# A block of sliding-window attention and a gated MLP: w_out's pieces made on GpSimd, w_in's second part in its own buffers, an inversion moved by one step, and the last two tiles' transposes inside products

## Chip, cores and metric

One core of one Trainium2 chip. The metric is the device time of one execution in microseconds (us), as the median of a few runs; profiles give a span (first to last instruction) on the same core.

## What is computed

Cut to what matters, for S = 2048 tokens of width D = 640, 32 heads of 20, a window of 256 and a hidden width of 2 x 864:

```python
h  = x + attention(layernorm(x)) @ wo        # causal, window 256, 32 heads
z  = gelu(layernorm(h) @ w_in)               # 2048 x 1728
z1, z2 = z[:, :864], layernorm(z[:, 864:])
g  = w_sp @ z2 + b_sp[:, None]               # a 2048 x 2048 matrix over the tokens
h2 = h + (z1 * g) @ w_out
```

All in fp32. The kernel takes one precise product as three: each operand is split into a high part, rounded to fp32r, and a low part, the operand less the high part, and hi·hi + hi·lo + lo·hi are summed.

## The kernel before

**Tiles and stages.** The tokens are 16 tiles of 128 (NT). The work goes through these stages, with the times of the profiled execution: v, q, k and attention (to about 462 us); the output projection with the second layernorm (to 550); z1, the first half of the hidden layer, by `z_pair` for eight pairs of tiles (550 to 641); z2 by `z2_pair` for pairs 8 to 12 (641 to 698); the first gates, which multiply w_sp's one half by the z2 that is ready (`first_gate`, 698 to 832); z2 of pairs 13 to 15 (832 to 868); the second gates, with the product by w_out between them (`second_gate`, 868 to 1116).

z1 and the gates use a scheme of seven block products in place of eight. Its right-hand pieces B11, T1, T2, B22, T3, B21 and T4 are made from four blocks by `right_blocks` (L724): high parts by copies on ScalarE (ACT, recorded at the helper's L720), low parts and block differences by subtractions on VectorE (DVE, L714).

**Who sets the order.** Up to the end of attention the order on each engine is that of the program. Behind `ms.close()` the framework's scheduler, with a timeline of its own, sets the order of every engine and of the DMA issues, so an edit there can shift many rows. Loads and stores are nearly all issued by SyncE (SP), some by GpSimd (POOL). Each engine works through its instructions in order. `steps` holds the matmul groups of the later stages, and `at(n, f)` places f at step n; `run(n)` does what is placed there and then step n.

**w_in's first half.** `win1_prep` (L771) makes the pieces of w_in for z1 while the projection's tiles pass: one `next` of it after each tile, two after each odd one. wraw is one buffer of [128, 2, 2, 432]. `load_win1(0, b)` puts the k-rows 0 and 2 of w_in there early (L208 to 210); after their pieces, rows 1 and 3 are loaded over them (`load_win1`, recorded at L193), and then row 4 (L783). Around them on ACT and DVE stand the projection's own operations for tile i: the layernorm's sums and its result hn(i) (L1249 to L1257), the split xb of the attention output for the tile after the next (L171 to L174), and ho, the copy of the transposed tile out of the bank ht_ps (L841 the transposes on PE, L720 the copy).

**The inversion.** `inverse_sums(c)` (L376) loads the softmax sums of 512 tokens from o_d, takes their reciprocals and stores these to r_d, from where `load_o`'s `load_rs` (L153) loads them spread over the partitions, as the factor for the attention output (`norm_o`, L163). It is a generator that takes one `next` in each step of attention: for c = 0 the reciprocal comes at the fourth. `proj_early(s)` places the first tiles' loads and splits into the last steps of attention; at s = 121 it loads both the outputs and the inverses of pair 1.

**w_out.** `second_gate(0)` loads the seven row blocks of w_out (128 x 640 each) into stage and row3, and splits each there: the high part by ACT (L136), the low part by DVE (L137), into e1["wout"], which lies in memory that the z2 weights hold until the last `z2_pair`. `staged_pieces` (L999) is work of the same kind that POOL already does in the first gates: it loads blocks of z2, makes their pieces in stage by a cast and a subtraction, and stores them to zp_d.

**The end.** `turn_y(n, dst)` (L1113) transposes tile n's z1·g and splits it into dst; `project` (L1126) multiplies by w_out; `final(n)` (L1139) adds h and stores. After the last step: `turn_y(14)`, `final(14)`, `turn_y(15)`, the last projection out_l.

## Time and profile before

| what | us |
|---|---|
| runs, median (lowest, highest) | 1122.15 (1116.82, 1125.29) |
| profiled execution, its own time | 1121.05 |
| its span | 1119.3 |
| TensorE (PE) busy | 1088.3 |
| DVE busy | 715.4 |
| ACT busy | 573.9 |
| POOL busy | 336.4 |
| DMA, mean rate over the span | 162 GB/s |

In the profile's timeline a row is: start, duration, engine, line, operation, out<-in, count, and in brackets how long the engine had stood idle before it and what ended that. A row of the list of waits is: waiting instruction <- releaser: total us, times, longest. A row of a table of stretches is: stretch, its length, then busy us (and instructions) of PE, of PE's weight loads, of DVE, ACT and POOL, the granted TensorE clock, the share of time that the DMA engines were busy, and GB/s. The names of the buffers are cut: wraw, zl (pieces of w_in, later of z2), aw (left-hand pieces), fx (loads of w_sp and of transposed tiles), m (attention outputs on their way to the projection).

### The profile page before, as it was taken

To read this page: it belongs to the slowest core of one execution; us is meant where nothing else is said; L and a number is where in the kernel's file an instruction comes from. 1 tells how busy PE (TensorE), PEld (TensorE's weight loads), DVE (VectorE), ACT (ScalarE), POOL (GpSimd) and SP (SyncE) were. 2 spreads that over 40 slices of the span, in tenths; PEclk is the share of its full clock that TensorE was granted. 3 is DMA by queue.
4 is the path that set the end of the run, shared out by engine and by line. 5 is a ranking of instruction groups with operands and counts; after the bars stand their busy time and mean duration, and the time that the engine had idled before them with its cause. 6 is when DMAs were issued, how large, how long until landed. Compare 5 with 4: busy or idle time off the path is not lost.

```text
span 1119.3 us, 27705 instructions
## 1 busy us (share of the span) xinstructions
PE 1088.3 (97%) x10667; PEld 976.1 (87%) x10667; DVE 715.4 (64%) x2038; ACT 573.9 (51%) x1222; POOL 336.4 (30%) x492
## 2 busy tenths in 40 slices
PE   8999999999999999989999999999999999999998
PEld 7998877668777887789989999999989899999998
DVE  6541113889999998676567478565538975566542
ACT  4334333259888999566766566433336521222210
POOL 3114444457666778401100155333101000000000
PEclk9999999999999999999999999999999999999999
DMA  7213665666666663588665421545571664444331
GB/s 259 74 33 102 171 218 165 204 208 196 194 198 192 209 194 119 170 277 288 226 200 177 151 76 38 182 153 197 177 248 38 202 182 140 124 135 148 99 95 59
DMA packets 86692, 182.44 MB, mean 163 GB/s; under 512 B 11552, under 2 KB 47904, under 8 KB 82640
## 3 DMA queue, kind: packets, MB, share of 16 engines
q1 hardware_dynamic: 82864, 169.46, 47.3%
q0 software_dynamic: 1392, 5.97, 1.6%
q10 hardware_dynamic: 2304, 5.24, 1.2%
q8 instruction: 84, 1.38, 0.5%
q14 instruction: 48, 0.39, 0.1%
HBM read 119.54 MB, written 62.29 MB: 162 GB/s over the span
## 4 chain that ended last, share of the span: by engine, by line
PE 59%; DMA 5%; DVE 4%; ACT 2%; issue 1%; SPq 1%; POOL 1%; DVEq 0%; ACTq 0%; POOLq 0%
PE g L1091 22%; PE out_ps L1130 8%; PE zb L953 7%; PE pv L432 5%; PE bank L338 4%; PE bank L404 4%; PE wo_ps L95 2%; PE zx L901 2%; PE zv L901 1%; PE zy L901 1%; PE yt_ps L1119 1%; DMA wraw<-w_in_in 1%; DMA fx<-w_in_in 1%; DVE zl L714 1%; DMA m<-r_d 1%
## 5 line engine op out<-in xcount | busy, mean ns | idle before, releaser
L407 ACT ACTIVATE pt<-bank 128x384 f32<-128x384 f32 (+2 forms) x512 | 200.2, 492 | 14.7 <-PE bank L404 10.9
L1091 PE MATMUL g<-zl,aw 128*128 128x432 f32 x768 | 172.4, 359 | 1.8 <-DVE zl L714 1.2
L720 ACT ACTIVATE aw<-fx 128x512 fp32r<-128x512 f32 (+2 forms) x160 | 93.0, 595 | 156.2 <-PE g L1091 98.7
L350 DVE CUSTOM_DVE_ANT_0 junk<-bank,strip 128x288 bf16<-128x288 f32 x392 | 157.7, 454 | 3.9 <-PE bank L338 2.4
L1091 PEld LDWEIGHTS g<-zl,aw 128*128 128x128 f32 x768 | 143.3, 188 | 9.1 <-DVE zl L714 1.8
L1091 PE MATMUL g<-ze,aw 128*128 128x432 f32 x576 | 133.8, 361 | 1.4 <-ACT aw L720 0.7
L432 PE MATMUL pv<-pt,v_sb 128*32 128x192 f32 (+3 forms) x1984 | 127.5, 321 | 3.0 <-DVE ot L448 1.3
L714 DVE TENSOR_TENSOR aw<-fx,aw 128x512 fp32r<-128x512 f32 (+2 forms) x152 | 98.7, 658 | 27.0 <-ACT aw L720 26.1
L1091 PEld LDWEIGHTS g<-ze,aw 128*128 128x128 f32 x576 | 107.2, 188 | 7.9 <-ACT aw L720 1.5
L404 PE MATMUL bank<-slot 123*32 123x288 bf16 (+5 forms) x1536 | 107.0, 280 | 2.8 <-ACT pt L407 1.3
L409 POOL TENSOR_SCALAR_AFFINE_SELECT pt<-pt 128x512 f32<-128x512 f32 x128 | 82.4, 644 | 49.6 <-ACT pt L407 48.5
L1130 PE MATMUL out_ps<-wout,y_sp 128*128 128x320 f32 (+1 forms) x630 | 95.9, 309 | 0.4 <-ACT y_sp L136 0.4
L953 PE MATMUL zb<-win,aw 128*128 128x432 f32 x480 | 95.4, 359 | 0.0
L1130 PEld LDWEIGHTS out_ps<-wout,y_sp 128*128 128x128 f32 (+1 forms) x630 | 94.0, 188 | 1.2 <-ACT y_sp L136 0.7
L953 PEld LDWEIGHTS zb<-win,aw 128*128 128x128 f32 x480 | 89.9, 188 | 4.9 <-DVE aw L714 0.4
L338 PE MATMUL bank<-slot 120*32 120x288 bf16 (+2 forms) x1264 | 87.7, 283 | 2.2 <-issue 1.2
L538 DVE TENSOR_TENSOR rest<-qk,sg 128x512 f32<-128x512 f32 x40 | 27.6, 691 | 86.5 <-ACT sg L536 86.5
L412 POOL TENSOR_SCALAR_AFFINE_SELECT pt<-pt 128x512 f32<-128x512 f32 x112 | 73.4, 655 | 0.0
L404 PEld LDWEIGHTS <-slot 123*32 123x32 bf16 x1536 | 53.6, 96 | 17.8 <-issue 6.9
L432 PEld LDWEIGHTS pv<-pt,v_sb 128*32 128x32 f32 x1984 | 60.2, 110 | 9.0 <-POOL pt L412 3.7
L541 POOL TENSOR_TENSOR sg<-rest,sg 128x512 bf16<-128x512 f32 x40 | 46.6, 1164 | 69.7 <-ACT sg L540 62.1
L714 DVE TENSOR_TENSOR row<-g,row 128x432 f32<-128x432 f32 x80 | 47.9, 602 | 27.9 <-PE g L1091 22.5
(210 smaller groups left out, 2158.3 us busy)
## 6 DMA issues: line engine op xcount, KB each, us to landing
fx<-wsp_in SPq DMA_DIRECT2D x32, 512.0 KB
slot<-qk_d SPq DMA_DIRECT2D x72, 200.0 KB
qk_d<-sg SPq DMA_DIRECT2D x32, 384.0 KB
slot<-qk_d SPq DMA_DIRECT2D x72, 160.0 KB
fx<-hn_d SPq DMA_DIRECT2D x32, 320.0 KB
o_d<-ot SPq DMA_DIRECT2D x64, 128.0 KB
z_d<-row SPq DMA_DIRECT2D x18, 432.0 KB
g_d<-row SPq DMA_DIRECT2D x16, 432.0 KB
```

Of the source, the lines that this page charges most:

```text
L338: nc.tensor.matmul(ps[32 * j:32 * j + 32, :n], part(st, half, 120, 0, hh, q0, 32), part(st, half, 120, 1, hh, lo + skip * j, n), start=Tru ...
L350: nc.vector.tensor_tensor_reduce(out=junk[:, :n], in0=ps[:, :n], in1=keep, scale=1.0, scalar=NEG, op0=OP.add, op1=OP.max, accum_out=m_cols ...
L404: nc.tensor.matmul(ps[32 * i:32 * i + 32, b:e], part(st, half, 123, 1, hh, k0, 32), part(st, half, 123, 0, hh, kb * P + b, e - b), start=T ...
L407: nc.scalar.activation(pt[:, hh, :n], ps[:, :n], AF.Exp, scale=SCALE)
L409: nc.gpsimd.affine_select(out=pt[:, :, :P], in_=pt[:, :, :P], pattern=[[0, 4], [1, P]], base=0, channel_multiplier=-1, compare_op=OP.is_ge ...
L412: nc.gpsimd.affine_select(out=pt[:, :, 256:], in_=pt[:, :, 256:], pattern=[[0, 4], [-1, P]], base=-1, channel_multiplier=1, compare_op=OP. ...
L432: nc.tensor.matmul(ps[32 * hh:32 * hh + 32, a - 512 * c:b - 512 * c], v_sb[:, kb, v0:v0 + 32], pt[:, hh, a - kb * P:b - kb * P], start=fir ...
L714: (eng or nc.vector).tensor_tensor(out=out, in0=a, in1=b, op=op)
L720: nc.scalar.activation(out, a, AF.Copy)
L953: nc.tensor.matmul(b[0][:, :HF], a[t][:, x, kk], win2[0][:, y, kk, h * HF:(h + 1) * HF], start=kk + x + y == 0, stop=kk == KD - 1 and x == 1)
L1091: nc.tensor.matmul(ps, w[m][x][:, k], zc[k][m][:, y], start=start and k + x + y == 0, stop=stop and k == 3 and x == 1, skip_group_check=True)
L1130: nc.tensor.matmul(ps[j][:, :HD], src[:w, a, k, :], e1["wout"][:w, b, k, j * HD:(j + 1) * HD], start=(k == 0 and a + b == 0), stop=(k == K ...
```

## The change

The diff, cut to its core:

```diff
+    wout_d = dram.tile([P, 2, KF * D], F32, name="wout_d")
...
+    ones = const.tile([P, 2], F32, name="ones")
...
-    def load_win1(k, b):
-        src = w_in[:, :FH].rearrange("k (h c) -> k h c", h=2)
-        r = (k + 2 * b) * P
-        nc.sync.dma_start(mem["wraw"][:, b], src[r:r + P])
+    def load_win1(b):
+        nc.sync.dma_start(mem["wraw"][:, b], w_in[2 * b * P:(2 * b + 1) * P, :FH].rearrange("k (h c) -> k h c", h=2))
...
         if s == 121:
-            for f in load_o(1)[:2]:
-                f()
+            tiles, mem["rs"], _ = load_o(1)
+            tiles()
             mem["invert"]()
         if s == 122:
+            mem["rs"]()
             norm_o(0, nc.vector)
...
-            for _ in range(5 if c else 3):
+            for _ in range(5 if c else 4):
                 yield
...
-            copy(pieces()[m][:, 0], raw[m])
+            nc.scalar.activation(pieces()[m][:, 0], raw[m], AF.Copy, scale=one)
...
-        return rows[i % 4][:, :D] if i > 11 else view(fx, (i % 4 - 2 + i // 9 * 2) * D, D)
+        if i == NT - 1:
+            return stage.bitcast(F32).rearrange("p a b -> p (a b)")[:, :D]
+        return rows[2][:, :D] if i == NT - 2 else view(fx, (i % 4 - 2 + i // 9 * 2) * D, D)
...
     def win1_prep(raw):
         seven, last = win1
+        rest = [r.rearrange("p (h c) -> p h c", h=2) for r in rows[:2]]
+        def pieces(k, blocks, one):
+            return right_blocks(lambda: [s[k] for s in seven], *(b[:, h] for b in blocks for h in range(2)), one=one)
+        yield
+        for n, f in enumerate(pieces(0, [raw[:, b] for b in range(2)], 1.0)):
+            f()
+            if n == 2:
+                for b in range(2):
+                    nc.sync.dma_start(rows[b], w_in[(2 * b + 1) * P:(2 * b + 2) * P, :FH])
             yield
+        nc.sync.dma_start(raw[:, 0], w_in[4 * P:, :FH].rearrange("k (h c) -> k h c", h=2))
         yield
         yield
+        for f in pieces(1, rest, ones[:, 0:1]):
+            f()
+            yield
+        yield
         for j in range(2):
-            split(*two(last[j]), raw[:, 0, j])
+            hi, lo = two(last[j])
+            nc.scalar.activation(hi, raw[:, 0, j], AF.Copy, scale=ones[:, 1:2])
+            minus(lo, raw[:, 0, j], hi.bitcast(F32))
         yield
...
+    def staged_wout(c):
+        n = min(HF, KF * D - c)
+        hi, lo = (stage[:, k, :n] for k in range(2))
+        nc.gpsimd.dma_start(lo.bitcast(F32), w_out[:, c:c + n])
+        nc.gpsimd.tensor_copy(out=hi, in_=lo.bitcast(F32))
+        minus(lo, lo.bitcast(F32), hi.bitcast(F32), nc.gpsimd)
+        nc.gpsimd.dma_start(wout_d[:, :, c:c + n], stage.bitcast(F32)[:, :, :n])
...
+                if c == 1 and p == 7 and m == T4 and k == 2:
+                    turn_y(NT - 2, e1["y"])
...
-    def project(ps, js, src):
+    def project(ps, js, src, middle=None):
         for k in range(KF):
+            if k == 3 and middle is not None:
+                middle()
...
             for k in range(KF):
-                t = n0 + (2 * k if k < 4 else 2 * k - 4)
-                at(t, lambda k=k: load_wout(k))
-                at(t + 2, lambda k=k: put_wout(k))
+                at(n0 + 1 + 3 * k // 2, lambda k=k: nc.sync.dma_start(e1["wout"][:, :, k].bitcast(F32), wout_d[:, :, k * D:(k + 1) * D]))
...
+    for i, c in enumerate(range(0, KF * D, HF)):
+        at(3 + 8 * i if i < 7 else len(steps) + 32 + 2 * i, lambda c=c: staged_wout(c))
...
+        if i in (3, 8):
+            nc.vector.tensor_scalar(out=ones[:, i // 8:i // 8 + 1], in0=mv[:, 3:4], scalar1=1.0, scalar2=1.0,
+                                    op0=OP.max, op1=OP.min)
...
     n = NT - 2
-    turn_y(n, e1["y"])
-    final(n)
-    turn_y(n + 1, y_sp2)
+    final(n, lambda: turn_y(n + 1, y_sp2, "a"))
```

- **w_in.** Rows 1 and 3 go into rows[0] and rows[1], buffers of their own, and their load is written right behind the third of the seven groups of the first part; row 4 goes into wraw when the first part's pieces are made. The high copies of the second part and of row 4 carry a scale of ones, which is clamped to 1 out of the statistics of tiles 3 and 8: it leaves the values as they are and ties those copies behind these statistics in the order. hn(15) moves from row3 to stage, hn(14) stays in row2.
- **The inversion** of c = 0 takes its reciprocal at the fifth `next`, and the load of pair 1's inverses moves from s = 121 to s = 122.
- **w_out.** The host lays w_out out as [128, 7·640] (each partition's rows of the seven blocks side by side). POOL makes its pieces in 11 chunks of up to 432 columns by way of stage, each with a load, a cast, a subtraction and a store to wout_d: seven at steps 3, 11, ..., 51, four behind `staged_pieces`. `second_gate(0)` only loads the pieces, [128, 2, 640] for each block; on SP these seven loads stand close together, behind the load of the first gate's g and the two z1 loads, where before the loads of w_out wait for their buffers. ACT's seven copies and DVE's seven subtractions go.
- **The end.** `turn_y(14)` is written into the last gate product, `turn_y(15)` into the middle of `final(14)`, with banks of the other tag.

How the instructions move, at the places where this is more than the diff shows. Names carry the tile's name and a serial number: m1 and xh are the projection's attention outputs and x tiles, inv the inverses.

ACT in the projection, where the second part's high copies stand, before (the tile's statistics L1252, xb L173, ho2 the copy that PE waits for):

```order
L1252 ACTIVATE m1_8948,mvc4_9813<-xh4_9587,mvc4_9813 128x640
L720 ACTIVATE zl1_9595<-wraw_8955 128x432
L173 ACTIVATE xb0_98<-m1_8948 128x640
L720 ACTIVATE zl7_9601<-wraw_8955 128x432
L720 ACTIVATE zl11_9605<-wraw_8955 128x432
L1257 ACTIVATE fx_9617<-xh3_8952,mvc3_9749 128x640
L1253 DMA h_d_68<-xh0_8949 128x640
L1257 ACTIVATE m1_8948<-xh4_9587,mvc4_9813 128x640
L720 ACTIVATE ho2_9590<-ht_ps2_9862 128x640
L720 ACTIVATE zl3_9597<-wraw_8955 128x432
L1252 ACTIVATE m1_8948,mvc5_9870<-xh0_8949,mvc5_9870 128x640
```

and now (rows 0 and 1 are the new buffers; L1266 the statistics):

```order
L1266 ACTIVATE m1_8950,mvc4_9823<-xh4_9589,mvc4_9823 128x640
L730 ACTIVATE zl1_9597<-row0_9612,ones_83 128x432
L730 ACTIVATE zl7_9603<-row1_9613,ones_83 128x432
L730 ACTIVATE zl11_9607<-row1_9613,ones_83 128x432
L175 ACTIVATE xb0_100<-m1_8950 128x640
L1274 ACTIVATE m1_8950<-xh4_9589,mvc4_9823 128x640
L721 ACTIVATE ho2_9592<-ht_ps2_9869 128x640
L730 ACTIVATE zl3_9599<-row0_9612,ones_83 128x432
L1267 DMA h_d_68<-xh0_8951 128x640
L730 ACTIVATE zl9_9605<-row0_9612,ones_83 128x432
```

The copies read row0 and row1 in place of wraw, and ho2 stands behind three of them as before.

SP in the projection, where the load of rows 1 and 3 stands, before (L193, with the load of w_in's second half, L792, above it):

```order
L387 DMA r_d_67<-inv1_8954 32x4x128
L155 DMA m1_8948<-r_d_67 128x1x256
L792 DMA fx_9617<-w_in_in 128x864
L149 DMA m1_8948<-o_d_66 128x1x256 x2
L141 DMA xh1_8950<-x_in 128x640
L149 DMA m1_8948<-o_d_66 128x1x256
L843 DMA hn_d_70<-ho0_9588 128x640
L149 DMA m1_8948<-o_d_66 128x1x256 x2
L155 DMA m1_8948<-r_d_67 128x1x256
L193 DMA wraw_8955<-w_in_in 128x864 x2
```

and now (L786 the same rows, L788 row 4):

```order
L388 DMA r_d_67<-inv1_8956 32x4x128
L786 DMA row0_9612<-w_in_in 128x864
L786 DMA row1_9613<-w_in_in 128x864
L157 DMA m1_8950<-r_d_67 128x1x256
L803 DMA fx_9619<-w_in_in 128x864
L157 DMA m1_8950<-r_d_67 128x1x256
L143 DMA xh1_8952<-x_in 128x640
L151 DMA m1_8950<-o_d_66 128x1x256 x3
L854 DMA hn_d_70<-ho0_9590 128x640
L151 DMA m1_8950<-o_d_66 128x1x256 x2
L788 DMA wraw_8957<-w_in_in 128x864
```

Rows 1 and 3 went ahead of the load L803 of w_in's second half, and row 4 stands about where they stood.

SP at the end of attention, with the store of the first inverses (L387 and L388), before:

```order
L149 DMA m1_8948<-o_d_66 128x1x256 x5
L383 DMA inv0_8953<-o_d_66 128x1x128
L387 DMA r_d_67<-inv0_8953 32x4x128
L449 DMA o_d_66<-ot7_1_0_9270 128x256
L449 DMA o_d_66<-ot7_1_1_9273 128x256
L149 DMA m1_8948<-o_d_66 128x1x256 x5
L155 DMA m1_8948<-r_d_67 128x1x256
```

and now:

```order
L151 DMA m1_8950<-o_d_66 128x1x256 x5
L384 DMA inv0_8955<-o_d_66 128x1x128
L450 DMA o_d_66<-ot7_1_0_9270 128x256
L450 DMA o_d_66<-ot7_1_1_9273 128x256
L151 DMA m1_8950<-o_d_66 128x1x256 x5
L388 DMA r_d_67<-inv0_8955 32x4x128
L384 DMA inv1_8956<-o_d_66 128x1x128
L157 DMA m1_8950<-r_d_67 128x1x256
```

The store r_d<-inv0 went from ahead of two o_d stores and five loads to behind them.

PE at the end, now (yt_ps14 and yt_ps15 the transposes of the last two tiles, g1_7 the last gate's products, L1153 the projection):

```order
L1112 MATMUL g1_7_0_0_14738<-zl8_9604,aw_9618 128x432 x3
L1112 MATMUL g1_7_0_0_14738<-zl15_9611,aw_9618 128x432 x3
L1140 MATMUL yt_ps14_0_14956<-ident_77,z1_0_13112 128x128 x4
L1140 MATMUL yt_ps14_4_14963<-ident_77,z1_0_13112 128x128 x2
L1140 MATMUL yt_ps14_4_14963<-ident_77,z1_0_13112 96x128
L1153 MATMUL out_ps14_0_14980<-wout_13110,y_sp_13111 128x320
L1153 MATMUL out_ps14_1_14981<-wout_13110,y_sp_13111 128x320
L1153 MATMUL out_ps14_0_14980<-wout_13110,y_sp_13111 128x320
L1153 MATMUL out_ps14_1_14981<-wout_13110,y_sp_13111 128x320
L1140 MATMUL yt_ps15_0_15000<-ident_77,z1_1_13113 128x128 x4
L1140 MATMUL yt_ps15_4_15007<-ident_77,z1_1_13113 128x128 x2
L1140 MATMUL yt_ps15_4_15007<-ident_77,z1_1_13113 96x128
L1153 MATMUL out_ps14_0_14980<-wout_13110,y_sp_13111 128x320
```

yt_ps14 stands behind the last of the gate's products, as it did before; yt_ps15, which before stood behind all 42 products of out_ps14, stands behind the first four.

31 lines of the change are left out of this document (8 added, 23 removed).

## Prediction

> **What bounds the kernel now.** I read the page's first line, then the list of what TensorE (PE) waited for, stretch by stretch, and then the timelines of the engines it waited for.
>
> ```profile
> PE 1088.3 (97%) x10667; PEld 976.1 (87%) x10667; DVE 715.4 (64%) x2038; ACT 573.9 (51%) x1222; POOL 336.4 (30%) x492
> PE ht_ps L841 <- ACT ho L720: 5.6, 3, 3.1
> PE pv L432 <- DVE ot L448: 1.3, 1, 1.3
> PE wo_ps L95 <- DVE xb L174: 1.0, 1, 1.0
> ...
> PE g L1091 <- DVE zl L714: 1.2, 2, 1.0
> PE g L1091 <- ACT zl L720: 0.6, 1, 0.6
> PE g L1091 <- ACT aw L720: 0.3, 1, 0.3
> ```
>
> PE is busy for 1088.3 of 1119.3 us, so 31 us of waiting and whatever a lowered clock costs is all that any rearrangement can win; the change takes no product away. The first three waits lie between 440 and 640 us (end of attention, output projection, first hidden-layer products), the last three between 860 and 910 (start of the second gates). They make 10.0 us, and the change touches each.
>
> **w_in's second part in its own memory.** Before, rows 2 and 4 of w_in (and then the last, row 5) are loaded over the one buffer wraw, after its former content has been used up. What that does is in the timelines of SP, ACT and PE:
>
> ```profile
> 484.26 0.50 SPq L792 DMA_DIRECT2D fx<-w_in_in  x1
> 492.22 1.06 SPq L193 DMA_DIRECT2D wraw<-w_in_in  x2
> 499.39 0.56 ACT L720 ACTIVATE zl<-wraw 128x432 fp32r<-128x432 f32 x1 [4.34 <-DMA wraw<-w_in_in]
> 503.75 1.33 PE L841 MATMUL ht_ps<-ident,fx 128*128 128x128 f32 x5 [3.07 <-ACT ho L720]
> 519.92 1.02 ACT L136 ACTIVATE zl<-wraw 128x432 fp32r<-128x432 f32 x2 [4.37 <-DMA wraw<-w_in_in]
> 521.58 0.76 PE L841 MATMUL ht_ps<-ident,fx 128*128 128x128 f32 x5 [1.83 <-ACT ho L720]
> 488.51 0.76 PE L841 MATMUL ht_ps<-ident,m 128*128 128x128 f32 x5 [0.74 <-ACT ho L720]
> ```
>
> The load is issued at 492.22 and lands near 499.3. ACT stands 4.34 us before the copy that needs it; the ho copy is queued some 3 us behind that, PE cannot overwrite ht_ps before it and stands 3.07 us until 503.75. The same happens with the last part: 4.37 us on ACT, 1.83 on PE. The changed order puts the loads of row0 and row1 just ahead of the load of w_in's second half, which before is issued at 484.26, and uses them no earlier than 495, so some 11 us lie between where 7 were needed; the last part is issued around 492 and used around 515. I count both waits as gone: 3.07 + 1.83 = 4.9. The 0.74 has another cause, a chain of statistics ahead of ho, and I leave it. The larger wait has a tail, in the table of stretches (column after POOL: granted clock):
>
> ```profile
> 504.00:506.00 2.00, 2.00 (x10) 2.00 (x10) 2.00 (x4) 2.00 (x5) 0.00 (x0) 0.50 0.90 267
> 506.00:508.00 2.00, 2.00 (x13) 2.00 (x13) 2.00 (x6) 0.51 (x2) 0.78 (x1) 0.81 0.98 382
> 522.00:524.00 2.00, 2.00 (x17) 2.00 (x15) 1.63 (x5) 1.18 (x4) 0.55 (x1) 1.00 0.70 236
> ```
>
> At 0.50 for 2 us and 0.81 for 2 us, PE loses 2 x 0.50 + 2 x 0.19 = 1.4 us; after the 1.83 us wait nothing is lost (1.00). Sum of this part 4.9 + 1.4 = 6.3. Its bounds: 7.0 with the 0.74, and about 3 if later loads take the place of these, since the DMA engines are busy for 0.70 to 0.98 here and the same bytes still pass. I take 6.3, because ACT's other idle stretches here end with DVE or PE, not with a load.
>
> The Trainium skill ("TensorE: Matmul & The Clock Gate", section "Why this matters for your kernels") says that an idle gap over about 3 us brings the half clock back. The trace agrees on both waits, 3.07 us with and 1.83 without a loss; by the page's window of about 3.4 us at half rate the loss would be some 1.7 us, an estimate, and the sum 0.3 larger.
>
> **The inversion one step later.**
>
> ```profile
> 455.69 0.95 DVE L386 RECIPROCAL inv<-inv 128x128 f32<-128x128 f32 x1 [5.86 <-DMA inv<-o_d]
> 456.56 0.69 DVE L448 COPY ot<-pv 128x256 f32<-128x256 f32 x2
> 456.67 0.58 SPq L387 DMA_DIRECT2D r_d<-inv  x1
> 457.35 1.01 SPq L449 DMA_DIRECT2D o_d<-ot  x2
> 458.41 4.12 SPq L149 DMA_DIRECT2D m<-o_d  x5
> 458.06 1.64 ACT L407 ACTIVATE pt<-bank 128x384 f32<-128x384 f32 x4 [0.77 <-PE bank L404]
> 466.32 1.56 DVE L165 TENSOR_TENSOR m<-m 128x640 f32<-128x640 f32 x2 [2.57 <-DMA m<-r_d]
> ```
>
> VectorE (DVE) waits 5.86 us for the softmax sums, with the two ot copies queued behind; PE needs one of them and stands the 1.3 of the first list. Now the copies come first. ACT, which sets attention's pace, stood only 0.77, so I count 0.8. The price: the store of the inverses went out on SP at 456.67, ahead of two o_d stores and five loads (1.01 + 4.12 us of queue); now it follows them, near 462, and the load of what it stores, which needs it landed, follows that, so the product at 466.32 starts 1.5 to 2 us later. Tile 2's split then ends near 472 instead of 470, and PE takes it up at about 471 to 472. I charge 0.3. Of the 1.0 on xb, the same kind of chain two tiles on (at 483.7), I count half. Sum 0.8 + 0.5 - 0.3 = 1.0; bounds 2.3 (both waits whole) and -1.0.
>
> **w_out by GpSimd.** Seven ACT copies and seven DVE subtractions leave the start of the second gates.
>
> ```profile
> 870.00:875.00 5.00, 4.19 (x21) 3.36 (x19) 2.58 (x9) 3.57 (x6) 0.55 (x1) 1.00 1.04 385
> 880.76 0.81 DVE L137 TENSOR_TENSOR wout<-stage,wout 128x640 fp32r<-128x640 f32 x1
> ...
> 882.66 0.66 PE L1091 MATMUL g<-zl,aw 128*128 128x432 f32 x2 [1.02 <-DVE zl L714]
> 900.64 0.74 PE L1130 MATMUL out_ps<-wout,y_sp 128*128 128x320 f32 x4
> ```
>
> The subtraction of 0.81 us and one like it 10 us earlier stand ahead of the 1.02 us wait, one copy and one subtraction ahead of the others of the first list: 1.2 + 0.6 + 0.3 = 2.1, of which I take 2.0 (bounds 0 and 2.2). The ready pieces are now loaded, 4.6 MB instead of 2.3, from about 868. With what else is loaded there (7.4 MB in all) that is 19 us at the best rate of this stretch, 385 GB/s, and 25 at 300: landed by 893, and first used at 900.64, so hidden. What pays is the place where GpSimd (POOL) makes the pieces: 11 chunks of load, cast, subtraction and store, seven under the first hidden-layer products (560 to 621), four after its present chunks of that kind:
>
> ```profile
> 759.64 0.55 POOL L1006 DMA_DIRECT2D stage<-z_d  x1 [3.93 <-DMA zp_d<-stage]
> ...
> 768.49 0.55 POOL L1006 DMA_DIRECT2D stage<-z_d  x1 [2.44 <-DMA zp_d<-stage]
> ...
> 789.23 0.56 POOL L1014 DMA_DIRECT2D zp_d<-stage  x1 [0.30 <-POOL stage L714]
> 833.01 1.56 POOL L714 TENSOR_TENSOR aw<-fx,aw 128x640 fp32r<-128x640 f32 x1 [43.22 <-DMA g_d<-row]
> ```
>
> A chunk takes 768.49 - 759.64 = 8.9 us, so the four end near 792 + 4 x 8.9 = 828, ahead of POOL's next work at 833.01. The seven lie in a stretch where POOL stood idle, DVE is busy 49.6 of 81 us and DMA 0.51 to 0.59:
>
> ```profile
> 560.00:600.00 40.00, 39.16 (x199) 36.50 (x198) 26.60 (x54) 26.19 (x48) 0.00 (x0) 1.00 0.59 190
> 600.00:641.00 41.00, 41.00 (x211) 39.28 (x210) 23.01 (x48) 23.38 (x44) 1.60 (x1) 1.00 0.51 164
> ```
>
> They bring 4.6 MB more (56 GB/s) and POOL beside DVE. PE idles only 0.84 here now; I charge 1.0, between 0 and 6 (rival 3).
>
> **The last two tiles' transposes.**
>
> ```profile
> 1101.68 6.67 PE L1130 MATMUL out_ps<-wout,y_sp 128*128 128x320 f32 x42 [0.42 <-ACT y_sp L136]
> 1108.19 0.93 PE L1119 MATMUL yt_ps<-ident,z 128*128 128x128 f32 x7
> 1109.48 6.57 PE L1130 MATMUL out_l<-wout,aw 128*128 128x320 f32 x42 [0.36 <-ACT aw L136]
> ```
>
> The transposes of tile 15 move from 1108.19 to behind the first four products of out_ps14; the splitting then lies under the other 38, and the 0.36 goes. In the order of the instructions those of tile 14 have not moved at all: they stand behind all of the last gate's products as before, so the 0.42 stays. I count 0.4 (bounds 0.2 and 0.9).
>
> **Sum**, on the profiled execution: 6.3 + 1.0 + 2.0 - 1.0 + 0.4 = 8.7 us off its 1121.05, 1112.35. It lies 1.1 below the median of the runs, 1122.15, so against that median 1113.45, or 1113.5.
>
> **Rivals.**
> 1. All of it comes: 7.0 + 2.3 + 2.2 + 0.9 = 12.4, nothing lost under the hidden-layer products. 1122.15 - 12.4 = 1109.8. For it: PE's waits name just these releasers. Against: one tight stretch after the other, so what is released meets the next limit.
> 2. The stalls move. Projection's DMA share stays at 0.70 and above, so half of the first part returns as a wait on other loads, the inversion gives nothing (its 0.8 was ACT's, its store is later): 3.1 + 1.5 + 0.4 - 1.0 = 4.0, 1118.1.
> 3. GpSimd's chunks disturb DVE. From the two timelines:
>
> ```profile
> 850.78 1.82 POOL L714 TENSOR_TENSOR aw<-fx,aw 128x640 fp32r<-128x640 f32 x1 [3.17 <-ACT aw L720]
> 851.19 1.87 DVE L714 TENSOR_TENSOR ze<-row,ze 128x432 fp32r<-128x432 f32 x1
> 852.99 0.59 DVE L714 TENSOR_TENSOR zl<-row,zl 128x432 fp32r<-128x432 f32 x1
> ```
>
> A subtraction beside a POOL operation took 1.87, one without 0.59: 1.3 us. With two operations in each of seven chunks that is 18 us of DVE, and if PE sees a third, 6: 8.7 + 1.0 - 6.0 = 3.7, 1118.4. Against: DVE has 31 us to spare there. The Trainium skill ("SBUF — State Buffer", section "Who interferes with whom") has this as a rule, a two-input DVE operation and a reading GpSimd operation shut each other out for a whole instruction; the rows above agree.
>
> 4. Slower: the four late chunks hold up POOL. The low half of pair 13's second tile (833.01) is needed by about 838, so POOL must be free by 836.4, that is (836.4 - 792) / 4 = 11.1 us a chunk. Beyond, PE stands four times the excess; at 13.3 us the whole gain is gone, at 14.5 the time is 1113.5 + 13.6 = 1127. Chunks of 8.9 us under the same loads speak against it.
>
> **How the numbers follow.** My forecast 0.35, rival 1 0.27, rival 2 0.25, rival 3 0.08, rival 4 0.05. The likeliest is 1113.5. The range goes from 1107 (rival 1 less some 2.8 us, for small waits that no part counts) to 1121 (rivals 2 and 3 and some 3 us above them); rival 4 stays out. About 1% is what a measurement of this kernel can tell from no change, 1110.9 being the bound: faster takes most of rival 1 and a little of my own, 0.28; slower is rival 4, 0.05; the rest 0.67.
>
> **What would show it.** Right: no ACT wait on a w_in load between 490 and 522, ht_ps waits under 1 us, the clock at 1.00 in 500 to 510; no pv wait on ot; no g wait of 1 us after 868; out_l following out_ps without a gap; POOL's last store before 833. Wrong: ho or xb waits of the same length with another load ahead of them, PE idle over 3 us between 560 and 641, or PE waiting at the start of the z products near 838.

## The result, and the profile after

The changed kernel is slower: 1129.32 us (median of 20 runs, 1120.54 to 1134.18) beside 1119.62 us of the kernel before (20 runs on the same chip, 1114.68 to 1125.29), a ratio of 1.0078 with a 95% interval of 1.006 to 1.0095. The prediction was 1113.5 in a range of 1107 to 1121. The profiled execution of the changed kernel took 1127.55 us, its span is 1125.9.

The page's first line of the kernel after, then the list of what PE waited for, over the whole span (waiting instruction <- releaser: total us, times, longest):

```profile
PE 1091.3 (97%) x10667; PEld 978.0 (87%) x10667; DVE 716.4 (64%) x2033; ACT 567.8 (50%) x1215; POOL 372.0 (33%) x536
...
PE ht_ps L852 <- ACT ho L721: 7.0, 4, 3.9
PE g L1112 <- ACT zl L730: 4.5, 2, 4.2
PE zx L912 <- DVE mvc L1263: 2.6, 1, 2.6
```

PE has the same 10667 products but is busy for 3 us more; products take longer at a lowered clock. Of the entries that the prediction lists, the wait of pv on ot (1.3), that of wo_ps on xb (1.0) and the gates' wait on DVE's zl (1.2) are gone. But the waits on ho are 7.0 instead of 5.6, there is a wait of 2.6 on mvc (0.7 before), and the second gates wait 4.2 us in one piece for ACT's zl, where that wait was 0.6.

To see where, I cut the spans at marks that every kernel has: the 470th exponential of attention, the first and the last product zx (the output projection ends and z1 starts at the first), the first gate product, the first and last z2 product of pairs 13 to 15, the last gate product, the end. One profiled execution each, us; the runs below are told in the next section.

| kernel | attention | projection | z1 | z2 | first gates | z2, late pairs | second gates | tail |
|---|---|---|---|---|---|---|---|---|
| before | 445.5 | 107.4 | 88.2 | 57.1 | 133.8 | 35.5 | 232.6 | 19.2 |
| after | 442.0 | 111.2 | 89.5 | 57.0 | 135.7 | 35.5 | 236.9 | 18.2 |
| wout_alone | 442.3 | 106.5 | 86.3 | 57.3 | 133.7 | 35.5 | 236.2 | 19.2 |
| late_h | 442.4 | 107.6 | 89.7 | 57.0 | 136.0 | 41.8 | 230.6 | 18.2 |
| nine | 445.9 | 106.4 | 89.9 | 56.6 | 138.2 | 35.4 | 230.6 | 18.2 |
| early_late | 444.9 | 106.9 | 88.4 | 57.2 | 133.9 | 35.4 | 230.7 | 18.2 |
| best | 440.7 | 106.4 | 89.3 | 57.0 | 133.7 | 35.5 | 230.6 | 18.2 |
| no_wout | 443.4 | 110.8 | 86.3 | 57.2 | 139.0 | 35.4 | 231.9 | 18.2 |
| no_wout_again | 441.9 | 110.7 | 86.4 | 57.2 | 133.9 | 35.4 | 232.4 | 18.2 |
| win_alone | 444.9 | 105.7 | 87.7 | 57.0 | 134.8 | 35.4 | 231.9 | 19.2 |
| win_no_rd | 443.1 | 102.3 | 87.8 | 57.0 | 133.8 | 35.4 | 231.9 | 18.2 |
| direct | 444.6 | 105.1 | 86.8 | 57.2 | 134.0 | 35.4 | 231.5 | 18.2 |

Attention scatters over 440 to 446 from one execution to the next, with the change or without. Against before, after loses 3.8 in the projection, 1.3 in z1, 1.9 in the first gates and 4.3 in the second gates, and wins 1.0 in the tail.

**The second gates.** The largest loss starts 50 us earlier, on POOL. Its timeline in the kernel after, the four late chunks of w_out (load at L1036, store at L1039):

```profile
794.53 0.54 POOL L1036 DMA_DIRECT2D stage<-w_out_in  x1 [2.50 <-DMA zp_d<-stage]
...
802.58 0.56 POOL L1036 DMA_DIRECT2D stage<-w_out_in  x1 [2.50 <-DMA wout_d<-stage]
...
813.99 0.56 POOL L1036 DMA_DIRECT2D stage<-w_out_in  x1 [5.80 <-DMA wout_d<-stage]
...
827.18 0.56 POOL L1036 DMA_DIRECT2D stage<-w_out_in  x1 [4.67 <-DMA wout_d<-stage]
834.00 0.71 POOL L1039 DMA_DIRECT2D wout_d<-stage  x1 [0.30 <-POOL stage L715]
```

From load to load they take 8.05, 11.41 and 13.19 us, not 8.9 (the fourth is a short one, of 160 columns instead of 432), and the last store goes out at 834.00. SP's timeline at that time, of the kernel after, and the row of the same loads of hn in the kernel before:

```profile
827.73 0.39 SPq L1031 DMA_DIRECT2D ze<-zp_d  x1
836.81 0.32 SPq L1160 DMA_DIRECT2D stage<-h_d  x1
...
838.98 1.40 SPq L973 DMA_DIRECT2D fx<-hn_d  x2
```

```profile
831.50 1.71 SPq L962 DMA_DIRECT2D fx<-hn_d  x2
...
892.82 0.33 SPq L1137 DMA_DIRECT2D stage<-h_d  x1
```

SP issues nothing between 828.1 and 836.81. It stands at the first load of h (L1160), whose target is stage, the buffer of POOL's last chunk. In the kernel before this load went out at 892.82, behind the loads of w_out into the same buffer. Those loads are gone, and the scheduler has put it some 20 rows earlier, ahead of three loads of hn that it stood behind. SP's order, before and then after (it holds no times):

```
L1020 DMA ze_10531<-zp_d 128x864
L962 DMA fx<-hn_d 128x640 x2
...
L1198 DMA stage<-w_out_in 128x640
L1198 DMA row_9613<-w_out_in 128x640
L1183 DMA row_9610<-g_d 128x864
L1137 DMA stage<-h_d 128x640
```

```
L1031 DMA ze_10536<-zp_d 128x864
L1160 DMA stage<-h_d 128x640
L1031 DMA ze_10533<-zp_d 128x864
L1126 DMA g_d<-row_9613 128x864
L1031 DMA ze_10535<-zp_d 128x864
L973 DMA fx<-hn_d 128x640 x2
```

Behind it wait the loads of hn, 838.98 instead of 831.50, and so on down the engines; timelines of ACT and PE in the kernel after:

```profile
846.19 0.74 ACT L721 ACTIVATE aw<-fx 128x640 fp32r<-128x640 f32 x1 [6.55 <-DMA fx<-hn_d]
...
880.58 1.37 PE L1112 MATMUL g<-zl,aw 128*128 128x432 f32 x2 [4.21 <-ACT zl L730]
```

ACT stands 6.55 us for the load and is behind with its copies until PE, 34 us later, runs out of zl and stands 4.21. The table of stretches there (stretch, length, busy us of PE, weight loads, DVE, ACT, POOL, granted clock, DMA share, GB/s):

```profile
880.00:882.00 2.00, 1.42 (x3) 1.04 (x4) 1.44 (x3) 1.44 (x5) 0.00 (x0) 0.50 0.96 325
882.00:884.00 2.00, 2.00 (x6) 1.32 (x6) 2.00 (x5) 1.07 (x2) 0.00 (x0) 0.50 1.03 411
884.00:886.00 2.00, 2.00 (x7) 1.85 (x6) 2.00 (x5) 1.09 (x2) 0.00 (x0) 0.50 1.04 420
886.00:888.00 2.00, 2.00 (x10) 1.88 (x10) 2.00 (x4) 0.00 (x0) 0.00 (x0) 0.86 0.99 352
```

The clock is halved for 6.8 us. Where PE was busy, that costs 1.42 x 0.5 + 2 x 1.0 + 0.28 = 3.0 us on top of the 4.21.

**The projection.** No wait on a w_in load stands between 490 and 522 any more, as predicted, and yet PE waits more. ACT's timeline, DVE's and PE's around 486 in the kernel after:

```profile
482.86 1.56 DVE L167 TENSOR_TENSOR m<-m 128x640 f32<-128x640 f32 x2 [1.74 <-issue]
484.97 0.56 ACT L730 ACTIVATE zl<-wraw 128x432 fp32r<-128x432 f32 x1 [2.54 <-DVE wraw L715]
...
486.81 1.00 PE L852 MATMUL ht_ps<-ident,m 128*128 128x128 f32 x5 [3.90 <-ACT ho L721]
...
527.35 0.77 PE L852 MATMUL ht_ps<-ident,m 128*128 128x128 f32 x5 [1.93 <-ACT ho L721]
```

DVE's product of the attention outputs with the inverses stands ahead of the subtraction that a w_in piece needs, ACT stands 2.54 us for the piece with ho queued behind it, and PE stands 3.90. This is not one of the two waits that the prediction counted. It stands at the second tile's transposes, where before has the 0.74 us at 488.51 that the prediction left aside. The two that were counted, at the fourth and the seventh tile (3.07 and 1.83 before), have shrunk; PE's timeline in the kernel after:

```profile
499.00 0.77 PE L852 MATMUL ht_ps<-ident,fx 128*128 128x128 f32 x5 [0.24 <-ACT ho L721]
...
515.46 0.77 PE L852 MATMUL ht_ps<-ident,fx 128*128 128x128 f32 x5 [0.95 <-ACT ho L721]
```

So 3.7 of the 4.9 us of w_in's waits went, and with them the half clock behind the first. The longer wait at the second tile, the new one at the ninth (527.35) and the 2.6 on mvc, two of them with a fall of the clock, took more than that. The stretches behind the 3.90 and the 1.93 us:

```profile
488.00:490.00 2.00, 2.00 (x9) 2.00 (x8) 1.56 (x9) 0.94 (x3) 0.90 (x1) 0.50 0.97 340
...
528.00:530.00 2.00, 2.00 (x11) 2.00 (x10) 1.64 (x5) 2.00 (x7) 0.79 (x1) 0.54 0.87 292
530.00:532.00 2.00, 2.00 (x11) 2.00 (x10) 2.00 (x8) 1.58 (x3) 0.00 (x0) 0.61 0.50 193
```

### The profile page after: what moved, and what is told of

Its sections match the earlier page's. It is cut to its first block, busy times and chain, and to the rows that moved or that the text cites. A ratio compares the mean times of both kernels' runs of the same rounds, so it can differ in the third digit from the quotient of the medians.

```text
span 1125.9 us, 27727 instructions
## 1 busy us (share of the span) xinstructions
PE 1091.3 (97%) x10667; PEld 978.0 (87%) x10667; DVE 716.4 (64%) x2033; ACT 567.8 (50%) x1215; POOL 372.0 (33%) x536
## 4 chain that ended last, share of the span: by engine, by line
PE 73%; DMA 9%; DVE 5%; issue 4%; ACT 4%; POOL 3%; SPq 2%; ACTq 0%; POOLq 0%; DVEq 0%
PE g L1112 19%; PE zb L964 8%; PE out_ps L1153 8%; PE pv L433 6%; PE bank L405 5%; PE bank L339 5%; DMA fx<-hn_d 3%; PE qk L523 2%; PE qk L524 2%; DMA fx<-wsp_in 2%; PE qk L525 2%; POOL sg L542 2%; PE wo_ps L97 2%; PE zx L912 1%; ACT pt L408 1%
## 5 line engine op out<-in xcount | busy, mean ns | idle before, releaser
L721 ACT ACTIVATE aw<-fx 128x512 fp32r<-128x512 f32 (+3 forms) x160 | 92.2, 594 | 186.7 <-PE g L1112 113.4
L715 DVE TENSOR_TENSOR aw<-fx,aw 128x512 fp32r<-128x512 f32 (+3 forms) x152 | 100.0, 670 | 29.9 <-ACT aw L721 28.6
L405 PE MATMUL bank<-slot 123*32 123x288 bf16 (+6 forms) x1536 | 106.9, 280 | 1.5 <-issue 0.6
L1153 PE MATMUL out_ps<-wout,y_sp 128*128 128x320 f32 (+1 forms) x630 | 96.6, 309 | 0.4 <-ACT y_sp L138 0.4
L1153 PEld LDWEIGHTS out_ps<-wout,y_sp 128*128 128x128 f32 (+1 forms) x630 | 94.3, 188 | 1.0 <-ACT y_sp L138 0.7
```

The source lines that it names most:

```text
L405: nc.tensor.matmul(ps[32 * i:32 * i + 32, b:e], part(st, half, 123, 1, hh, k0, 32), part(st, half, 123, 0, hh, kb * P + b, e - b), start=T ...
L715: (eng or nc.vector).tensor_tensor(out=out, in0=a, in1=b, op=op)
L721: nc.scalar.activation(out, a, AF.Copy)
L1153: nc.tensor.matmul(ps[j][:, :HD], src[:w, a, k, :], e1["wout"][:w, b, k, j * HD:(j + 1) * HD], start=(k == 0 and a + b == 0), stop=(k == K ...
```

## The experiments

Two theories on the second gates: SP's queue is held by the load of h (theory 1, Q in the expectations), or POOL is late itself, the prediction's fourth rival (both together are G). Each run has a ratio to the kernel before on its own chip, with its 95% interval.

**Which part is slow.** wout_alone is the kernel before with the w_out part only, no_wout the changed kernel without it, win_alone and inv_alone the kernel before with one part each. Of the changed kernel's diff they have these lines:

```diff
 # wout_alone
+    def staged_wout(c):
...
+                at(n0 + 1 + 3 * k // 2, lambda k=k: nc.sync.dma_start(e1["wout"][:, :, k].bitcast(F32), wout_d[:, :, k * D:(k + 1) * D]))
 # win_alone, and in no_wout as well
+                    nc.sync.dma_start(rows[b], w_in[(2 * b + 1) * P:(2 * b + 2) * P, :FH])
 # inv_alone, and in no_wout as well
-            for _ in range(5 if c else 3):
+            for _ in range(5 if c else 4):
 # no_wout alone of the four
+    final(n, lambda: turn_y(n + 1, y_sp2, "a"))
```

> The kernel before with the w_out part alone; the first load of h into stage stands early on SP here too. Theory Q: 1126 to 1129, ratio 1.005 to 1.009, with the same ScalarE wait on fx<-hn_d ahead of the second gates. If the loss needs the other parts as well: 1118 to 1121, ratio under 1.002.

> The change without its w_out part: w_in's second part in own memory, the inversion one step later, the transposes at the end. Theory Q with stalls that move in the projection (ScalarE and VectorE wait for other loads of the same busy DMA engines): 1118 to 1122, ratio 0.998 to 1.003. As the prediction's terms have it (6.3 + 1.0 + 0.4 off): about 1112, ratio 0.993. If the loss is not in the w_out part at all: 1126 or more, ratio 1.006.

> The kernel before with w_in's second part in its own memory alone. As predicted: the two waits and the half clock gone, 6.3 off, about 1113.5, ratio 0.994. Rival (the stalls move to loads of the transposed tiles and of o_d, since the DMA engines stay at 0.8 to 0.9): 1117 to 1122, ratio 0.998 to 1.002, the waits on wraw gone and waits of 2 to 4 us on other loads in ScalarE's timeline between 515 and 555.

> The kernel before with the inversion one step later alone. Predicted: 1.0 us off, ratio 0.999, the TensorE wait of 1.27 us on ot near 457 gone. Rival (the later store of the first inverses is paid in the projection): ratio 1.001 to 1.004, the 1.27 gone all the same and longer waits of VectorE for m<-r_d and of TensorE on ho between 465 and 490.

Measured: wout_alone 1123.33, 1.004 [1.0018, 1.0062]; no_wout 1122.62, 1.0006 [0.9984, 1.0029]; win_alone 1116.8, 0.9973 [0.9952, 0.9995]; inv_alone 1119.62, 0.9994 [0.9976, 1.0013]. w_out's part alone is a loss, and for the rest without it none is measured. The scheduler put wout_alone's first seven chunks into the projection (472 to 560) and not under z1, so its z1 is one without chunks. Its four late chunks lie where the change has them, and the same chain stands, here on SP, ACT and PE:

```profile
819.76 0.37 SPq L1021 DMA_DIRECT2D ze<-zp_d  x1
827.92 0.32 SPq L1146 DMA_DIRECT2D stage<-h_d  x1
...
836.99 0.74 ACT L721 ACTIVATE aw<-fx 128x640 fp32r<-128x640 f32 x1 [6.47 <-DMA fx<-hn_d]
...
871.39 2.09 PE L1100 MATMUL g<-zl,aw 128*128 128x432 f32 x4 [4.04 <-ACT zl L721]
```

In win_alone the projection takes 105.7, 1.7 less than before, of the 6.3 that I had counted, and by the runs' ratio the part is worth 3.0 us (0.6 to 5.4). inv_alone has no wait of pv on ot any more, and its time can't be told from that of the kernel before; the interval reaches from 2.7 us faster to 1.5 slower. no_wout has a hold of the same kind as the one on SP, in the kernel before's own code, and its first gates take 139.0; the timelines of SP and PE:

```profile
789.59 0.32 SPq L1116 DMA_DIRECT2D g_d<-row  x1
795.80 0.33 SPq L1212 DMA_DIRECT2D stage<-w_out_in  x1
796.23 0.38 SPq L1051 DMA_DIRECT2D fx<-wsp_in  x1
...
802.86 0.86 PE L1103 MATMUL g<-ze,aw 128*128 128x432 f32 x3 [3.39 <-DVE row L714]
```

SP stands 5.9 us at a load of w_out into stage, which POOL's pieces of z2 hold, with a load of w_sp behind it, and PE then waits 3.39. Its repetition below has 133.9 there.

**Taking SP's wait away.** late_h ties the first load of h behind a load of z1 by a copy of one column on DVE, so that it goes out where it did before:

```diff
+        if p == 0:
+            at(n0 + 9, lambda: nc.vector.tensor_copy(out=e1["h"][0][:, :1], in_=e1["z1"][0][:, :1]))
         at(n0 + (9 if p == 0 else 6), lambda: load_h(i))
```

> The changed kernel, with one tiny VectorE copy more that makes the first load of h into stage wait for a z1 load, so that it stands on SP behind the loads of w_out's pieces and no longer ahead of the last z pieces and transposed tiles. Theory Q (that load, waiting on SP for GpSimd's last w_out store, holds up the loads behind it and so ScalarE and TensorE): ScalarE's wait of 6.55 us on fx<-hn_d near 846 goes, the TensorE wait of 4.21 us at the first second gate falls under 2 us, no half clock there, and the time falls by 4.2 + 3.4 of the changed kernel's 1129.3, to about 1121.5 (ratio to before 0.999 to 1.004). Rival R (the w_out chunks and the 4.6 MB of loads cost the time by contention, the queue only shows it): still 1127 or more, ratio 1.006 or more.

Measured: 1119.66, 1.0009 [0.9982, 1.0035]. From 1.0078 that is 0.0069 or 7.7 us (by the two intervals, give or take 3.5). SP loads hn at 832.99 and the second gates take 230.6, the 2.0 less than before that was predicted. But the profiled execution lost the late pairs of z2 instead, 41.8. POOL's and PE's timelines and the stretches of late_h:

```profile
797.32 0.54 POOL L1036 DMA_DIRECT2D stage<-w_out_in  x1 [3.94 <-DMA zp_d<-stage]
...
834.53 0.55 POOL L1036 DMA_DIRECT2D stage<-w_out_in  x1 [7.94 <-DMA wout_d<-stage]
...
841.35 3.14 POOL L715 TENSOR_TENSOR aw<-fx,aw 128x640 fp32r<-128x640 f32 x2
...
843.05 2.17 PE L964 MATMUL zb<-win,aw 128*128 128x432 f32 x5 [3.54 <-POOL aw L715]
```

```profile
842.00:844.00 2.00, 0.95 (x3) 0.90 (x4) 0.00 (x0) 0.00 (x0) 2.00 (x2) 0.50 0.25 88
...
848.00:850.00 2.00, 2.00 (x10) 1.88 (x9) 0.61 (x1) 1.84 (x3) 0.00 (x0) 0.84 0.00 0
```

Four chunks from 797.32 to 841.35 are 11.0 us each, and POOL's next work, which the prediction wanted begun by 836.4, begins at 841.35: PE stands 3.54 us and has 6.8 us of half clock. So both theories hold, one behind the other. The profiled execution took 1125.12 us, 5.5 above the median, and late_h's runs lie between 1113.83 and 1128.99. That POOL comes in time in the shorter ones would fit, but is not shown.

**Taking the late chunks away.** early_late places all 11 chunks closer and from the projection on, with the tie of h; hn(15) then needs a place outside stage. nine leaves two chunks late and puts nine early. best ties two chunks of the four to statistics of z2, so that POOL makes them in the first gates, and best_inv has the inversion's part too (early_late_no_inv leaves it out).

```diff
 # early_late, early_late_no_inv
-        at(3 + 8 * i if i < 7 else len(steps) + 32 + 2 * i, lambda c=c: staged_wout(c))
+        at(3 + 4 * i, lambda c=c: staged_wout(c))
...
-            return stage.bitcast(F32).rearrange("p a b -> p (a b)")[:, :D]
+            return rows[3][:, :D]
 # nine
+        at(3 + 6 * i if i < 9 else len(steps) + 32 + 2 * i, lambda c=c: staged_wout(c))
 # best, best_inv
+        if tie is not None:
+            nc.gpsimd.tensor_copy(out=lo.bitcast(F32)[:, :1], in_=tie)
...
+        late = {7: (81, 11, 1), 8: (85, 12, 0)}.get(i)
```

> The changed kernel with all 11 of GpSimd's w_out chunks placed early (steps 3, 7, 11, ...), hn(15) kept in row3 so that stage is free for them during the projection, and the first load of h tied behind a z1 load. Theory G (the whole loss behind 828 us comes from the four late chunks: through SP's queue in the changed kernel, through GpSimd's own queue once the load of h is moved): no TensorE wait over 2 us and no half clock between 828 and 900, and the time is that of w_in's part and the end with w_out's gain, 1112 to 1116, ratio 0.993 to 0.997. Rival: the chunks now stand between the projection's small GpSimd operations and their DMAs beside its loads, which costs as much: 1119 or more, with the tile's layernorm waiting for GpSimd in the projection.

> As early_late, with the inversion as it was before. If the inversion one step later gains what I predicted (1.0 us), this is 1 us slower than early_late. If it loses in the projection what it gains in attention (the part without w_out measured 1.0006, w_in alone 0.9973, the end takes 1.0 off): 2 to 4 us faster than early_late.

> The changed kernel with nine chunks in the first hidden-layer stage (one every six steps) and two late, and the load of h tied as in late_h; hn(15) in stage as in the changed kernel. Theory G: GpSimd's chain behind its z2 pieces is half as long and ends before 820, so no wait near 843 and no half clock there: 1115 to 1119, ratio 0.996 to 1.000, against 1.0009 of late_h. Rival: the two chunks more delay GpSimd's z2 work between 630 and 660 by more than they save: TensorE waits there of over 2 us and 1120 or more.

> w_in's part, w_out's part and the end on the kernel before, without the inversion's part; of the 11 w_out chunks seven under the first hidden-layer products as in the change, two tied (by a copy of one column from statistics of z2) to GpSimd's idle stretch at 692 to 710, two behind its z2 pieces; the load of h tied as in late_h. Theory G, by the parts as measured (w_in 3.0 off, the end 1.0, the second gates 2.0): 1112 to 1115, ratio 0.993 to 0.997, GpSimd done before 822, no TensorE wait over 1.5 us after 560. Rival: the disturbance under the first hidden-layer products and the two chunks at 700 cost as much as the second gates gain: 0.998 or more.

> The changed kernel with two of its four late chunks moved to 692 to 710 and the load of h tied: best with the inversion one step later. Theory G with an inversion worth nothing (inv_alone 0.9994): within 2 us of best. If the inversion is paid in the projection once w_in's part is there too: 2 to 5 us slower than best.

Measured: early_late 1114.57, 0.9958 [0.994, 0.9976], faster than both kernels; early_late_no_inv 1114.42, 0.996 [0.994, 0.9979]; nine 1121.19, 1.0027 [1.0007, 1.0048]; best 1118.09, 0.9991 [0.9974, 1.0008]; best_inv 1118.52, 0.9997 [0.9978, 1.0016]. All five profiles have 230.6 to 231.4 in the second gates; PE's waits of early_late from 826 to 1000:

```profile
PE g L1112 <- DVE row L715: 0.7, 1, 0.7
PE g L1112 <- ACT aw L721: 0.3, 1, 0.3
PE g L1112 <- DVE zl L715: 0.2, 1, 0.2
```

nine and best miss theory G's range. nine lost elsewhere: its eighth and ninth chunk (loads at 631.58 and 643.31) stand ahead of POOL's share of z2, and PE's timeline has a wait at the start of the first gates, which take 138.2. That the one comes from the other is argued, not shown:

```profile
707.37 1.88 PE L1112 MATMUL g<-ze,aw 128*128 128x432 f32 x8 [2.97 <-ACT aw L721]
```

Both pairs with and without the inversion's part differ by 0.0006 or less, and their intervals leave room for some 3 us either way. Why best has a longer median than early_late stays open. Their profiles don't tell it: best's is its shortest execution (1113.09 us) and early_late's (1117.33) lies 2.8 above its median; with chunks in the projection, early_late even had a wait of PE of 6.55 us at 491.84.

**What bounds the projection.** Two theories: loads (rival 2: DMA share above 0.7, the stalls move to the next load), or the way of the inverses (sums, reciprocal, store to r_d, load, product m), which stands ahead of w_in's pieces on DVE. win_tail is the w_in part with the tail; win_light is win_alone without the x loads from tile 5 on and without h's stores for them; win_no_rd is win_tail with the sums loaded in place of the inverses, with no wait for r_d, and no_wout_no_rd the same with the inversion's part (these three leave out work and compute something else); no_wout_again repeats no_wout beside it. direct keeps the computation: each pair's sums are loaded spread over the partitions and inverted there by DVE, and inverse_sums goes; direct_best and direct_early are best and early_late_no_inv with it.

```diff
 # win_light
+        if i < 5:
             nc.sync.dma_start(hs[i], x[i * P:(i + 1) * P, :])
...
+        if i < 5:
             nc.scalar.dma_start(h_d[i], xt)
 # win_no_rd, no_wout_no_rd
-        def load_rs(base=r_d[:, t], step=S):
+        def load_rs(base=o_d[:, DH, t], step=32 * S):
 # direct, direct_best, direct_early
-                    inverse.append(inverse_sums(c))
...
+            tiles, _, sums = load_o(i // 2 + 2)
+            mem["inv%d" % (i // 2 + 2)] = sums()
+            tiles()
+        if i % 2 == 0 and i + 2 < NT:
+            mem["inv%d" % (i // 2 + 1)]()
```

> win_alone with a third of the projection's DMA traffic left out: from tile 5 on x is not loaded (the buffers hold the sums of earlier tiles) and h not stored, and the end reads the h of the first five tiles. If the waits that took the place of those on wraw come from the DMA engines' load: TensorE's waits between 470 and 555 fall from win_alone's 5 us to under 2, no half clock there, and the time is 3 to 5 us under win_alone's, about 1112. If they come from the order of the instructions: the same waits and win_alone's time within 1.5 us.

> The kernel before with w_in's part and the end alone, w_out as before. As the sum of the parts: 3.0 + 1.0 off, 1115 to 1116, ratio 0.996 to 0.997. best less this is what w_out by GpSimd is worth when its chunks stand in idle stretches: 2 us faster by theory G, 0 to 2 slower by its rival.

> win_tail with the attention output multiplied by the softmax sums themselves, loaded from o_d, in place of their inverses from r_d: the way sums, reciprocal, store, load is left out from the second pair of tiles on (the reciprocals are still taken and stored). If that way is what bounds the projection once w_in's loads are out of it: from the 470th exponential of attention to the first product of the hidden layer 103 us or less, against 105.7 in win_alone and win_tail, and 2 us less in all. If the layernorm chain of each tile and the order of ScalarE's and VectorE's queues bound it: 105 to 106.5 and the same time within 1.5 us.

> The same with the inversion one step later as well (no_wout with the sums in place of the inverses). no_wout took 110.8 us for that stretch, each of its two parts alone 105.4 and 105.7. If the two parts together lose because the later inverses hold up VectorE, with w_in's subtractions queued behind: back to 103 to 106 and 3 to 5 us less than no_wout, ratio about 0.996. If something else in the new order loses it: 109 or more, ratio 1.000.

> no_wout once more, beside them on one chip. If its 110.8 us are the order's: 109 to 112 again and a wait of 3 to 4 us on ho near 488, ratio 0.999 to 1.003. If they were one execution's: 105 to 107, ratio 0.996.

> win_tail with every pair's softmax sums loaded straight from o_d over the partitions and inverted there (a VectorE reciprocal of 128 x 256 for each pair, 1.74 us as the first pair's), in place of the way by a reciprocal of 128 x 128, a store to r_d and a load back; all of the computation is kept. If the way of the inverses bounds the projection: 103 to 105 us for its stretch, against 105.7, the time 1113 to 1116, ratio 0.994 to 0.997. If VectorE's 12 us of reciprocals take its place: 106 or more, ratio 0.999 or more.

> best with the same direct way of the inverses. If the gains add: the 2 us of the second gates and the 2.3 us under the hidden-layer products cancel, as in best against win_tail, so within 2 us of direct.

> early_late_no_inv with the same direct way of the inverses. If its gain over best (0.996 against 0.999) came from the chunks standing in the projection and not under the hidden-layer products: 1 to 3 us under direct, ratio 0.992 to 0.995. If VectorE's reciprocals and GpSimd's chunks meet in the projection: slower than direct.

Measured: win_light 1117.89, 0.9993 [0.9971, 1.0016], projection 105.3 beside 105.7 of win_alone: fewer loads give next to nothing, which speaks against the first theory. win_tail 1115.97, 0.9989 [0.9966, 1.0012]; win_no_rd 1112.34, 0.9937 [0.9914, 0.9961], projection 102.3; no_wout_no_rd 1112.83, 0.9958 [0.9933, 0.9983], 103.3; no_wout_again 1119.4, 1.0 [0.9977, 1.0023], 110.7. So without the wait for the inverses some 3 to 7 us of the projection go, and at the second tile's transposes PE's wait on ho, 3.69 and 2.30 in no_wout and no_wout_again, is 0.72 in no_wout_no_rd. Both ends are in the rows, PE's list of win_no_rd from 462 to 556, where only a wait of 0.3 follows, and a product of no_wout_again on DVE:

```profile
PE ht_ps L850 <- ACT ho L719: 1.5, 2, 0.8
PE zx L910 <- DVE mvc L1262: 1.2, 1, 1.2
PE wo_ps L96 <- DVE xb L175: 0.9, 1, 0.9
```

```profile
473.62 1.56 DVE L166 TENSOR_TENSOR m<-m 128x640 f32<-128x640 f32 x2 [5.23 <-DMA m<-r_d]
```

direct, a lawful way to the same end, did not bring it: 1117.57, 0.9984 [0.9962, 1.0007], projection 105.1; direct_best 1115.71, 0.9972 [0.9951, 0.9992]; direct_early 1119.49, 1.0 [0.9979, 1.0021]. In the projection DVE takes eight reciprocals, most of 1.75 us, where win_tail has five, one of 1.74 and four of 0.95, and PE has a wait of 3.2 on ho and one of 2.7 on fx.

## Why the prediction was wrong, point by point

- **"A chunk takes 8.9 us, so the four end near 828, ahead of POOL's next work" failed**, and with it the gain. The pattern came from POOL's earlier pieces. In the new place one took 8.05 to 13.19 us in the kernel after, and 11.0 in the mean of late_h's four, and they began at 794.53 and 797.32 instead of 792. Removing the late chunks (late_h to early_late, 1.0009 to 0.9958) is worth 0.0051 or 5.7 us, give or take 3.6; early_late moves the other seven as well, so this is no price of the four alone.
- **"POOL's next work" was the wrong place to look: the step failed at SP.** I asked who waits for POOL as an engine and not who waits for the buffer that it fills. The load of h into stage is the first, it is SP's, and it had moved some 20 rows up; the order of the changed kernel showed that before any run. late_h shows its price, 7.7 us.
- **Rival 4 had the right mechanism and place, with a chance much too low** (0.05): in late_h's profile POOL comes late to the low half of the second tile of pair 13. Its threshold of 11.1 us a chunk was not passed, with 11.0; POOL was free 5 us after the 836.4 because its chunks also began 5 us later than the 792 of the sum. It was not what decided in the profile of after, where SP's hold came first and POOL's next operation, at 835.95, waited for ACT.
- **w_in, "I count both waits as gone": 6.3 was mis-sized.** The loads did go out in time and the two waits shrank, but only 1.7 us came in the profile (win_alone), and in the seven executions with the inversion's part as well the projection takes 105.9 to 111.2, beside 107.4 before. The stalls moved, as rival 2 had it, but to the way of the inverses, not to loads: win_light and win_no_rd tell these apart. Why 105.9 to 111.2, and what bounds the projection at 102 to 105, stay open.
- **The inversion, 1.0: not measurable, and its price was looked for in the wrong place.** inv_alone 0.9994, early_late with and without it 0.9958 and 0.996; a gain of 1.0 us lies within these intervals, as does none. The 1.3 on ot and the 1.0 on xb are gone in after, but the wait that I left aside as one with another cause, on ho at the second tile's transposes, is 1.58 to 6.55 us in all eight profiles with this part and the inverses from r_d. In those without it that have the inverses from r_d it is 0.74 or less, and with this part but without the wait for r_d it is 0.72 (no_wout_no_rd). I charged 0.3 for all of this.
- **w_out's second gates, 2.0: right by the row of before**, once nothing holds SP: 232.6 to 230.6 in late_h, nine, best and best_inv. Kernels without this part have 231.5 to 232.6, so it is 0.9 to 2.0.
- **Disturbance under z1, 1.0: too small beside the runs without it.** z1 takes 88.6 to 89.9 where the seven chunks lie there and 86.3 to 87.8 in the later runs with none there, some 2.4 in the mean; before itself had 88.2, which leaves 0.4 to 1.7. DVE's groups from 560 to 630, before and after:

```profile
L714 DVE TENSOR_TENSOR fx<-fx 128x256 f32<-128x256 f32 x22 | 9.2, 420 | 5.1 <-DMA fx<-hn_d 4.8
L714 DVE TENSOR_TENSOR win<-fx,win 128x864 fp32r<-128x864 f32 x5 | 5.3, 1057 | 4.5 <-ACT win L720 4.4
```

```profile
L715 DVE TENSOR_TENSOR fx<-fx 128x256 f32<-128x256 f32 x22 | 11.6, 528 | 9.4 <-DMA fx<-hn_d 9.1
L715 DVE TENSOR_TENSOR win<-fx,win 128x864 fp32r<-128x864 f32 x5 | 6.2, 1243 | 6.1 <-ACT win L721 6.1
```

The subtractions take 528 ns instead of 420 and 1243 instead of 1057 (2.4 + 0.9 us in all), and the wait for hn loads grows by 4.3 us: which of the chunks' operations and bytes does it was not told apart. The 6 us of rival 3 were not seen.
- **The tail, 0.4: 1.0** in every profile with the edit (19.2 to 18.2).

Together: the forecast's gain was 0.0078 of the time, the result a loss of 0.0078. Of these 0.0156, by the differences of the ratios, each good to some 0.003, 0.0069 is SP's hold, 0.0051 the late chunks (with the move of the other seven), and the rest, 0.0036 or 4.0 us, is put down to the projection, z1 and the inversion's part, which gave less than counted.

## What to carry to other kernels

When work moves to another engine, list every later instruction that touches its buffer, on each queue, and look in the new order for what now stands ahead of them: a load that waits for its buffer holds all loads behind it in the queue. Price a chunk of load, work and store by the loads of the stretch it moves to, and give a mechanism with a threshold of 11.1 us more than 0.05 when the only price, 8.9, comes from another stretch. Where a wait is taken away on a path with several tight chains, count on the next chain unless its slack is in a row.

## What the runs showed of the hardware

A wait's length does not decide what it costs in clock. In the kernel after, 1.93 us at 527.35 has 0.54 and 0.61 behind it, 1.7 us lost, while in before 1.83 us at 521.58 cost nothing. wout_alone lost as much after 1.72 us (at 482.0), and nine lost nothing after its 2.97 and no_wout nothing after 3.69 (at 488.0).

The clock's own times tell why. In the kernel after it is halved from 487.20, 528.16 and 879.73 on, for 3.41, 3.41 and 6.83 us, and these starts lie 12 and 103 steps of 3.41 us apart. In every profile with more than one such start they lie on such a grid, with an offset that differs from profile to profile. Here are stretches cut along the grid, of before, after and no_wout in this order, with the columns as above:

```profile
520.37:523.78 3.41, 2.20 (x16) 2.20 (x17) 2.54 (x7) 2.60 (x6) 0.55 (x1) 1.00 0.67 234
```

```profile
524.76:528.17 3.41, 1.48 (x12) 1.22 (x11) 2.80 (x7) 2.71 (x4) 0.00 (x0) 1.00 0.70 230
```

```profile
482.77:486.18 3.41, 1.58 (x11) 1.32 (x9) 2.09 (x4) 0.78 (x1) 0.00 (x0) 1.00 0.91 313
486.18:489.60 3.42, 1.56 (x12) 1.56 (x13) 3.42 (x8) 3.05 (x6) 0.00 (x0) 1.00 0.87 304
```

The 1.93 us fall whole into one step and leave PE busy for 0.43 of it, and the next step is at half clock. The 1.83 us fall into two steps, of which the emptier one keeps 0.65, and the 3.69 us into two of 0.46 each. From 460 us to the last gates, in the 20 profiles of all kernels here, a half clock began behind each of the 24 steps in which PE was busy for less than 0.44 and behind none with more than 0.47; in between it went either way. So what a wait of 1.7 to 3.7 us costs beyond itself depended here on where it fell on the grid. It was nothing, or 1.7 us for one step at half clock (also after the 4.04 us of wout_alone), or 2.8 to 3.0 where two steps followed, as after the 3.54 of late_h and the 4.21 of after.

The rule of the Trainium skill that the prediction cites ("TensorE: Matmul & The Clock Gate", section "Why this matters for your kernels"), a gap of over about 3 us, does not hold here, neither for the 1.93 us with a loss nor for the 3.69 without; the measurement decides.
